# Narrowing fewer pieces of the channel weights while the first batch's attention runs alone

## The chip, the cores and the metric

One core of a Trainium2 chip runs the whole program. The metric is the device time of one execution in microseconds (us). The kernel before took 1027.16 us, the median of three runs that lay between 1025.83 and 1028.11. Its engines are TensorE (PE in the profile, with PEld for its weight loads), VectorE (DVE), ScalarE (ACT), GpSimd (POOL) and SyncE (SP), which here issues the loads and stores.

## The reference

Four batches of 576 tokens go through three layers: an attention with 8 heads of width 64 in which only scores within `tau` of the row's maximum count, a mixing layer, and a routed layer with 8 experts.

```python
scores = scale * np.matmul(q, k.transpose(0, 1, 3, 2))
thresh = np.max(scores, axis=-1, keepdims=True) - tau
scores = np.where(scores >= thresh, scores, -1000000000.0)
scores = scores - np.max(scores, axis=-1, keepdims=True)
attn = np.exp(scores)
attn = attn / (np.sum(attn, axis=-1, keepdims=True) + 1e-09)
x = np.matmul(attn, v)

h = x.transpose(0, 2, 1) @ U @ V            # mixing along the tokens
u = x + h.transpose(0, 2, 1)
x = u + np.maximum(u @ w_ch1, 0.0) @ w_ch2  # the channel layer, 512 -> 2048 -> 512
# then: each token picks an expert e, or keeps the one of the token before it
out = p[e] * (np.maximum(x @ w1[e], 0.0) @ w2[e])
```

`U`, `V`, `w_ch1` and `w_ch2` arrive as eight-byte floating-point numbers, everything else in four bytes. The change bears on `w_ch1` and `w_ch2`, which are called the channel weights here.

## The kernel before, in words

The program has stages. **Stage 0** is the attention of batch 0 by itself (`attention_alone`). **Stage 1** runs the attention of batch 1 beside the channel layer of batch 0 (`attention(1)` and `channel(0)`), stages 2 and 3 do the same for the next batches, and the routed experts come last.

In stage 0 the attention goes over 36 tiles of scores (4 pairs of heads, 9 tiles each) in a loop over `i`, from 0 to 38. For a tile, TensorE makes scores (L321, L323), VectorE finds the row maximum (L356, tile `st`), ScalarE takes the exponential (L367, tile `p`), VectorE masks (L371), TensorE transposes (L427) and ScalarE copies the result out of PSUM (L428, tile `ptt`), and TensorE multiplies with V (L446 to L450, tile `po`). The next pair of heads is loaded beside that: a load into `raw`, a cast `kh` on ScalarE (L292), a remainder `kl` (L293, on GpSimd for these pairs) and a cast `qs` (L300). Where a tile leaves TensorE idle, matmuls that compute nothing (L596, `idle`) are put in.

**Narrowing.** Matmuls need four-byte weights, so a generator `convert` turns the eight-byte numbers into four-byte ones, piece by piece. Every `next(conv)` is called a call here. A call issues the load of a new piece into `cr` (L204), casts the piece of the call before on ScalarE (L212, tile `top`) and joins the piece of two calls before on VectorE (L219, tile `w`). The join's result is stored to a buffer `wdram` in HBM (L243). There are 35 pieces: one for U, two for V, and two for each of the 16 blocks `f` of the channel weights, so that block `f` is pieces 4 + 2f and 5 + 2f. The first of the two holds the weights of the first matrix, the second those of the second. `cr` has three buffers. Casts and joins are pinned (`keep_in_program_order`): the planner can't move them on their engines. A piece that is joined has been read out of `wdram` again before it can be used: `load_w(b, f)` loads a block into `wr` (L686), splits it into a high part `w0h` or `w1h` (on ScalarE, L693, for blocks 0 and 1 of batch 0, on GpSimd, L691, for the later ones) and a low part `w0l` or `w1l` (L694, on GpSimd). `w0h` and `w0l` have two buffers.

What calls when: in stage 0 the loop over `i` keeps a `debt` that decides at which `i` a call is made. `load_w(0, f)` makes as many calls as are missing until `DONE` has reached `f`; that is the case at call 8 + 2f. In stage 1 the rest of the calls stand beside attention and channel layer in `interleave`, which lets each generator go forward by its share of the whole; the calls' share is set as if there were 30. `channel(0)` begins with `load_w(0, 0)` and `load_w(0, 1)`, computes the first layer of block 0 (`mlp_l1`, L715 to L717, tile `l`; relu L718, L719), then calls `load_w(0, 2)`, and so on. In between, after each fourth block, comes the second layer (`mlp_l2`, L730 to L732).

A planner puts the instructions of every engine in an order from the order in which they were traced and from its own estimates of what is ready when. In stage 0 GpSimd alone keeps the traced order. Loads of `wr` are often moved to well before the place where they were traced.

Of the kernel before, what the change touches and what calls it, by code (L numbers as in the profile page):

```python
# [103 lines left out]
def attention_channel_moe(ctx, tc, qk, vv, tau, umat, vrep, wch, wgl, wexp, consts, out):  # L104
# [765 lines left out]
    debt = 0  # L870
    with tc.manual_schedule(engines={mybir.EngineType.Pool}):
        for i in attention_alone(0):
            if i >= 4:
                debt += 0.2 if i > 9 else 1
                while debt > 0:
                    next(conv, None)
                    debt -= 1
# [514 lines left out]
```

## Time and profile before

| what | value |
|---|---|
| median of three runs | 1027.16 us |
| profiled execution | 1030.32 us |
| its span, first to last instruction | 1028.5 us |
| PE busy | 992.5 us (97%) |
| DVE busy | 714.4 us (69%) |
| ACT busy | 612.9 us (60%) |
| POOL busy | 156.3 us (15%) |
| TensorE's granted clock, mean | 0.996 |

The profiled execution took 1.82 us more than its span, which is the time before the first and after the last instruction. All times in rows count from the span's start. Busy time is a sum over stages that have different limits, so the shares in the table do not say which engine a stage waits for; the rows by stage do. Stage 0 ends at 109.56 us, where the first matmul of the channel layer starts, and stage 1 ends near 262 us.

### The profile page before, as it was taken

The numbers are of one execution on the slowest core, as the hardware profiler recorded it, in microseconds if no ns is written. First come the engines' busy times: TensorE is split into PE (matmuls) and PEld (weight loads), VectorE is DVE, ScalarE is ACT, GpSimd is POOL, SyncE is SP. The second block draws the span as 40 slices with busy tenths as digits, with TensorE's granted clock in tenths as the row PEclk, the third lists the DMA queues.
The fourth block names the chain that finished last, engine by engine and source line by source line (L and its number), as shares of the span: only waits on it lengthen the run. The fifth ranks groups of instructions, "written<-read, shape, count | busy, mean of one in ns | idle before, by whom it ended". The sixth has DMA issues, their size and how long they took to land.

```text
span 1028.5 us, 17792 instructions
## 1 busy us (share of the span) xinstructions
PE 992.5 (97%) x6309; PEld 831.9 (81%) x6310; DVE 714.4 (69%) x1764; ACT 612.9 (60%) x1250; POOL 156.3 (15%) x149
## 2 busy tenths in 40 slices
PE   8898999999999999999999999999999899999996
PEld 4676777778787787788889888999998798889884
DVE  7898687786777877777686655682469655566673
ACT  6888687676587776776475553432353344355562
POOL 3322345332000000000000000014400321120100
PEclk9999999999999999999999999999999999999999
DMA  7655486863332322323111011362243645565550
GB/s 229 226 157 178 155 267 222 277 213 111 121 104 95 103 86 81 114 98 99 52 58 52 33 52 39 132 234 94 82 161 144 232 147 185 173 194 197 194 184 16
DMA packets 58529, 143.72 MB, mean 140 GB/s; under 512 B 7421, under 2 KB 8573, under 8 KB 58432
## 3 DMA queue, kind: packets, MB, share of 16 engines
q1 hardware_dynamic: 55072, 132.27, 39.5%
q0 software_dynamic: 3360, 10.23, 3.0%
q8 instruction: 52, 0.85, 0.3%
q14 instruction: 45, 0.37, 0.1%
HBM read 124.65 MB, written 18.61 MB: 139 GB/s over the span
## 4 chain that ended last, share of the span: by engine, by line
PE 75%; DVE 6%; ACT 5%; DMA 4%; issue 4%; POOL 1%; SPq 0%; POOLq 0%; DVEq 0%; ACTq 0%
PE l L730 6%; PE l L732 6%; PE l L731 6%; PE l L715 6%; PE l L717 5%; PE l L716 5%; PE tp L427 4%; PE el L1211 4%; PE el L1258 3%; PE el L1257 3%; PE el L1213 3%; PE el L1256 3%; PE el L1212 3%; PE po L446 3%; PE s L321 3%
## 5 line engine op out<-in xcount | busy, mean ns | idle before, releaser
L1142 ACT ACTIVATE eh<-ew 128x512 fp32r<-128x512 f32 x160 | 94.2, 627 | 70.1 <-PE el L1258 55.5
L1143 DVE TENSOR_TENSOR el<-ew,eh 128x512 fp32r<-128x512 f32 x160 | 106.9, 692 | 40.6 <-ACT eh L1142 38.1
L371 DVE SCALAR_TENSOR_TENSOR p<-s,st,p 128x576 f32<-128x576 f32 x144 | 114.0, 815 | 19.8 <-ACT p L367 16.0
L715 PE MATMUL l<-uh,w0h 128*128 128x256 f32 (+2 forms) x352 | 126.7, 361 | 0.3 <-ACT yT L519 0.3
L367 ACT ACTIVATE p<-s,st 128x576 f32<-128x576 f32 x144 | 103.4, 738 | 32.2 <-DVE st L356 30.9
L716 PE MATMUL l<-ul,w0h 128*128 128x256 f32 (+2 forms) x352 | 122.6, 348 | 0.0
L717 PE MATMUL l<-uh,w0l 128*128 128x256 f32 (+2 forms) x352 | 122.3, 348 | 0.0
L356 DVE TENSOR_REDUCE st<-s 128x1 f32<-128x576 f32 x144 | 105.3, 751 | 16.1 <-PE s L323 15.2
L730 PE MATMUL l<-hh,w1h 128*128 128x512 f32 (+3 forms) x320 | 115.4, 361 | 0.0
L732 PE MATMUL l<-hh,w1l 128*128 128x512 f32 (+3 forms) x320 | 112.6, 352 | 0.0
L731 PE MATMUL l<-hl,w1h 128*128 128x512 f32 (+3 forms) x320 | 112.2, 351 | 0.0
L428 ACT ACTIVATE ptt<-tp 128x512 f32<-128x512 f32 (+1 forms) x192 | 88.5, 489 | 31.0 <-PE tp L427 30.6
L694 POOL TENSOR_TENSOR w1l<-wr,w1h 128x512 fp32r<-128x512 f32 x24 | 31.4, 1320 | 453.7 <-DVE rha L1000 426.2
L321 PE MATMUL s<-kh,qs 128*128 128x288 f32 x320 | 95.7, 319 | 4.6 <-DVE p L371 4.5
L427 PE MATMUL tp<-cst,p 128*128 128x128 f32 x576 | 91.7, 276 | 5.5 <-ACT ptt L428 4.2
L735 DVE TENSOR_TENSOR yT<-l,yT 128x448 f32<-128x448 f32 (+2 forms) x96 | 50.1, 522 | 58.5 <-PE l L732 57.9
L323 PE MATMUL s<-kl,qs 128*128 128x288 f32 x320 | 88.7, 296 | 0.0
L381 ACT ACTIVATE p<-p,rv 128x576 f32<-128x576 f32 x108 | 78.6, 771 | 15.9 <-DVE rv L391 15.7
L427 PEld LDWEIGHTS tp<-cst,p 128*128 128x128 f32 x576 | 68.0, 140 | 21.7 <-ACT ptt L428 10.1
L446 PE MATMUL po<-ptt,v 128*64 128x256 f32 (+1 forms) x256 | 70.2, 413 | 2.8 <-ACT ptt L435 2.0
L447 PE MATMUL po<-ptt,v 128*64 128x256 f32 (+1 forms) x256 | 70.9, 414 | 1.7 <-ACT ptt L428 1.7
L715 PEld LDWEIGHTS l<-uh,w0h 128*128 128x128 f32 x352 | 66.4, 189 | 6.7 <-DVE rsm L810 0.7
(613 smaller groups left out, 2433.5 us busy)
## 6 DMA issues: line engine op xcount, KB each, us to landing
ew<-in_wexp_dram SPq DMA_DIRECT2D x80, 512.0 KB, 4.5
wr<-wdram SPq DMA_DIRECT2D x128, 256.0 KB, 2.9
cr<-in_wch_dram SPq DMA_DIRECT2D x32, 512.0 KB, 4.8
raw<-in_qk_dram SPq DMA_DIRECT2D x30, 304.0 KB, 3.1
wdram<-w SPq DMA_DIRECT2D x32, 256.0 KB, 3.1
v<-in_vv_dram SPq DMA_DIRECT2D x16, 352.0 KB, 4.1
raw<-in_qk_dram SPq DMA_DIRECT2D x16, 320.0 KB, 3.1
raw<-in_qk_dram SPq DMA_DIRECT2D x16, 288.0 KB, 4.1
```

The source lines that it names most:

```text
L321: pe.matmul(s["t"][:, h, :288], lhsT=qs[:, qc:qc + 128], rhs=kh[:, k0:k0 + 288], start=(j == 0), stop=False)
L356: dve.tensor_reduce(out=self.st[:, 0, h:h + 1], in_=self.t[h], axis=AX.XY, op=ALU.max, negate=True)
L367: act.activation(self.halves(h), self.t[h], AF.Exp, bias=self.st[:, 0, h:h + 1])
L371: dve.scalar_tensor_tensor(out=p, in0=self.t[h], scalar=self.st[:, 1, h:h + 1], in1=p, op0=ALU.is_ge, op1=ALU.mult, accum_out=self.rvs[:, ...
L427: pe.transpose(tp[:, c - c0], src[:, c * 128:c * 128 + 128], ident)
L715: pe.matmul(pm, lhsT=w1h[:, wk], rhs=uh[k], start=(k == 0), stop=False)
L716: pe.matmul(pm, lhsT=w1h[:, wk], rhs=ul[k], start=False, stop=False)
L717: pe.matmul(pm, lhsT=w1l[:, wk], rhs=uh[k], start=False, stop=(k == 3))
L730: pe.matmul(pm, lhsT=w2h[:, wd], rhs=xh, start=(f == f0), stop=False)
L731: pe.matmul(pm, lhsT=w2h[:, wd], rhs=xl, start=False, stop=False)
L732: pe.matmul(pm, lhsT=w2l[:, wd], rhs=xh, start=False, stop=(f == f0 + 3))
L1143: dve.tensor_tensor(out=lo, in0=x, in1=hi.bitcast(F32), op=ALU.subtract)
```

## The change

The debt grows by 0.1 instead of 0.2 for each `i` above 9.

```diff
     with tc.manual_schedule(engines={mybir.EngineType.Pool}):
         for i in attention_alone(0):
             if i >= 4:
-                debt += 0.2 if i > 9 else 1
+                debt += 0.1 if i > 9 else 1
                 while debt > 0:
                     next(conv, None)
                     debt -= 1
```

Worked through, the calls of stage 0 are made before at i = 4 to 10, 15, 20, 25, 30 and 35 (12 calls), and after at i = 4 to 10, 20 and 30 (9 calls). The remaining pieces are narrowed in stage 1, by the calls in `load_w` and in `interleave`. The number of pieces and the work on each are the same.

## Rows read from the trace of the kernel before

**Rows 1.** Busy by stage: us, PE, PEld, DVE, ACT, POOL; clock, DMA, GB/s.

```profile
0.00:109.50 109.50, 94.64 (x647) 66.77 (x648) 93.82 (x229) 90.06 (x196) 32.44 (x33) 1.00 0.61 190
109.50:262.00 152.50, 146.75 (x866) 112.91 (x867) 113.30 (x238) 109.87 (x209) 59.42 (x58) 1.00 0.67 214
262.00:430.00 168.00, 167.74 (x1016) 130.37 (x1016) 128.93 (x305) 124.42 (x256) 0.00 (x0) 1.00 0.31 101
```

**Rows 2.** VectorE, joins of i = 25 and 35: start, length, instruction, [idle before].

```profile
69.74 0.68 DVE L219 SCALAR_TENSOR_TENSOR w<-cr,top 128x512 int32<-128x512 int32 x1
...
93.23 1.51 DVE L219 SCALAR_TENSOR_TENSOR w<-cr,top 128x512 int32<-128x512 int32 x1
```

**Rows 3.** ScalarE in stage 0, three casts and what follows.

```profile
47.41 0.80 ACT L212 ACTIVATE top<-cr 128x512 f16<-128x512 bf16 x1
...
70.56 0.79 ACT L212 ACTIVATE top<-cr 128x512 f16<-128x512 bf16 x1
71.21 0.67 ACT L292 ACTIVATE kh<-raw 128x576 fp32r<-128x576 f32 x1
...
76.61 0.80 ACT L300 ACTIVATE qs<-raw,t 128x608 fp32r<-128x608 f32 x1 [0.31 <-DMA raw<-in_qk_dram]
...
93.96 0.79 ACT L212 ACTIVATE top<-cr 128x512 f16<-128x512 bf16 x1
...
97.20 0.80 ACT L300 ACTIVATE qs<-raw,t 128x608 fp32r<-128x608 f32 x1 [0.35 <-DMA raw<-in_qk_dram]
```

**Rows 4.** TensorE from 47 us on.

```profile
47.43 0.43 PE L447 MATMUL po<-ptt,v 128*64 128x256 f32 x1 [1.35 <-ACT ptt L428]
...
52.10 0.71 PE L427 MATMUL tp<-cst,p 128*128 128x128 f32 x5
```

**Rows 5.** The chain of waits: start, length, what.

```profile
71.96 1.43 POOL kl L293
...
73.40 3.18 DMA raw<-in_qk_dram
...
82.52 2.47 DMA wdram<-w
...
85.00 5.79 DMA wr<-wdram
...
92.79 1.42 POOL kl L293
```

**Rows 6.** VectorE as stage 1 begins.

```profile
110.35 0.75 DVE L671 TENSOR_TENSOR ul<-yT,uh 128x256 fp32r<-128x256 f32 x2
...
113.98 1.58 DVE L219 SCALAR_TENSOR_TENSOR w<-cr,top 128x512 int32<-128x512 int32 x2
```

**Rows 7.** Transfers issued in 115:135: KB each, median us to landing.

```profile
cr<-in_wch_dram SPq DMA_DIRECT2D x5, 512.0 KB, 4.3
wdram<-w SPq DMA_DIRECT2D x5, 256.0 KB, 3.1
wr<-wdram SPq DMA_DIRECT2D x4, 256.0 KB, 3.3
```

**Rows 8.** GpSimd, the first block split in stage 1.

```profile
112.42 0.61 POOL L691 CAST w0h<-wr 128x512 fp32r<-128x512 f32 x1 [16.25 <-PE l L716]
113.11 1.30 POOL L694 TENSOR_TENSOR w0l<-wr,w0h 128x512 fp32r<-128x512 f32 x1
```

**Rows 9.** TensorE around the layer of block 2.

```profile
116.69 0.40 PE L715 MATMUL l<-uh,w0h 128*128 128x512 f32 x1
...
117.81 0.48 PE L716 MATMUL l<-ul,w0h 128*128 128x512 f32 x1
...
120.41 0.27 PE L427 MATMUL tp<-cst,p 128*128 128x128 f32 x1
...
123.43 0.70 PE L450 MATMUL po<-ptt,v 128*128 128x256 f32 x2
```

**Rows 10.** Busy time of the first 20 us of stage 1.

```profile
110.00:130.00 20.00, 19.69 (x111) 15.59 (x110) 11.62 (x25) 13.43 (x25) 9.84 (x10) 1.00 0.61 196
```

## The prediction

> **What bounds the kernel now.** I read the busy time by stage first [rows 1], because shares over the whole span mix stages with different limits. The reader is to see three things there. In stage 0 no engine is full: of 109.5 us PE is busy 94.64, DVE 93.82 and ACT 90.06, so the stage is a chain that passes from engine to engine, and an instruction taken out of one of them pays only where the chain runs through it. In stage 1 PE is busy 146.75 of 152.5 us, so 5.75 us are idle and the stage is nearly PE's own. From 262 to 430 us PE is busy 167.74 of 168.0. What stage 0 and stage 1 win or lose together therefore arrives at the end, and nothing later gives it back.
>
> Then I read VectorE and ScalarE around the removed joins and casts [rows 2, 3], TensorE beside one of them [rows 4], the chain of waits through the second half of stage 0 [rows 5], and finally what stands at the start of stage 1 [rows 6 to 10], because that is where the moved pieces arrive.
>
> **What the change removes from stage 0.** Before, calls are made at i = 15, 20, 25, 30 and 35; after, at 20 and 30. Each call holds one cast and one join, so three casts and three joins leave. By place they are those of i = 15, 25 and 35; what stands at 20 and 30 stays there, on an earlier piece. A cast holds ScalarE for 0.65 us (70.56 to 71.21), a join VectorE for 0.68 [rows 2, 3].
>
> - i = 15: the cast at 47.41 lies beside TensorE, which starts at 47.43 on a PSUM copy and then runs through to the transposes at 52.10 [rows 3, 4]. The chain is on TensorE there, so I count nothing. Its cover gone, it would be the cast's 0.65.
> - i = 25: the cast at 70.56 stands directly ahead of the cast `kh` at 71.21, and behind that come `kl` on GpSimd (71.96, 1.43 us), the load of `raw` (73.40, 3.18 us) and the cast `qs` at 76.61, before which ScalarE sat idle for 0.31 us on that load [rows 3, 5]. If the whole run moves up by 0.65, `qs` is 0.31 earlier for certain, and more if the copies ahead of it move too. I take 0.5.
> - i = 35: the cast and the join lie at 93.96 and 93.23, but `qs` at 97.20 again waited for a load, which waits for the `kl` that starts at 92.79, ahead of both [rows 3, 5]. What is late next is that load, so the gain is small; I take 0.2.
>
> Stage 0 thus gives back 0.7 us. The bounds are 0, if all of it falls into waits, and three casts of 0.65 with joins of 0.68, 0.68 and 1.51, together 4.8 us. I stay near the lower end because two of the three places have a row that shows something else ending last.
>
> The join at 93.23 took 1.51 us where the one at 69.74 took 0.68, and `kl` ran on GpSimd from 92.79 to 94.21 beside it [rows 2, 5]. The Trainium skill has a rule for this (SBUF — State Buffer, Who interferes with whom): a DVE instruction with two inputs in SBUF contends with a GpSimd instruction that reads SBUF. It speaks against the change, since GpSimd is busy 32.44 of 109.5 us in stage 0 and 9.84 of 20 us where the pieces go [rows 1, 10]. By that rule the first moved join would take 0.83 us longer when it meets GpSimd, and the sum below would be 1028.8; without it, it is 1028.0.
>
> **What it adds to stage 1.** The three casts and three joins come back in its first 20 us: 2.0 us for each engine. DVE is idle for 8.4 and ACT for 6.6 of these 20 us [rows 10], so the work itself costs nothing; PE is busy for 19.69, so what counts is whether it is kept waiting. GpSimd's splits, the stores and the loads are the same in number.
>
> The weights come later. `load_w(0, 1)` needs call 10 and finds nine, so it makes one, and that call joins piece 8, the first half of block 2. Before, call 10 stood at i = 25, near 70 us. Now it stands behind `mix(0)`, whose last remainders `ul` end on VectorE at 111.10 [rows 6]. Shifted by the 0.7 from stage 0, that is 110.4. Then come the join (0.68), the store to HBM (3.1), the load back (3.3) and the split on GpSimd (112.42 to 114.41, 1.99) [rows 7, 8]: 119.5. The layer of block 2 issued its first matmul at 116.69 and the rest from 117.81 on [rows 9]; shifted, 117.1. The weights come 2.4 us late. The store took 2.47 and a load 5.79 in the chain [rows 5], which makes it 1.7 to 4.9.
>
> What hides part of it: the transposes and the product with V that run from 120.41 to 124.13 [rows 9] could go ahead of block 2, if the planner orders them so and the copies that they read are there. Whole cover would leave 0, no cover 4.9. I take 1.5 of the 2.4: the product's own inputs are copied while the wait lasts, so not all of it can move up.
>
> Behind that the schedule meets the old one. In `interleave` the calls get one turn for each 1/30 of the stage; before, `load_w(0, 4)` finds 16 calls made, as it needs, and after it finds 15 and makes one. From block 5 on the counts are the same, so blocks 3 and 4 are the last that can be late. Their pieces are joined before the layers of blocks 1 and 2, a block or two ahead, so I count 0 for them.
>
> A pinned cast can also hold up ScalarE. The buffer of piece 11 is freed by the join of call 10, at about 111.1, and its load takes 4.3 us [rows 7], so its cast can't start before 115.4, while its place, in call 12, is close behind block 0. Behind it queue the exponentials of batch 1 and the relus, for which TensorE and VectorE wait. ScalarE's 6.6 idle us cover it; if not, it costs up to 2.
>
> **The sum.** -0.7 + 1.5 = +0.8. Against the profiled execution's own time, 1028.5 of span and 1.82 around it, that is 1030.32 + 0.8 = 1031.1; the median of the runs is 3.16 us below that execution, so the median should be 1027.16 + 0.8 = 1028.0. About 0.2% (2.05 us) is what a measurement of this kernel can tell from no change, so this is within 1025.1 to 1029.2.
>
> **Rivals.**
>
> *Stalled at the head of stage 1 (slower).* The planner leaves block 2 where it was. TensorE takes its instructions in order, so the whole lateness is idle time. For: a load took 5.79 us in the chain [rows 5], and PE has 0.31 idle us in these 20 [rows 10]. Against: in stage 1 as a whole PE has 5.75 idle us [rows 1], part of which attention work done early can fill. It decides once the weights come later than the product with V can cover. Price: 4.9 - 0.7 = +4.2, so 1031.4.
>
> *Stage 0 pays in full (faster).* If the chain is carried by ScalarE and VectorE at all three places, and block 2 is covered, the gain is up to 4.8; with half of what the bound leaves above my 0.7 it is 0.7 + 2.05 = 2.75, so 1024.4. For: at 71.21 and 97.20 ScalarE waits by only 0.31 and 0.35 for loads [rows 3], so the two paths are almost equally long, and the moved work goes to engines that have 8.4 and 6.6 us free. Against: TensorE's run from 47.43 and the load chain.
>
> *It does nothing.* `load_w` makes missing calls, and loads of `wr` are moved early anyhow; if the store and load were never waited for and the casts were hidden, the time is 1027.2.
>
> **Chances and range.** Forecast 0.42, stall 0.27, full gain in stage 0 0.24, nothing 0.07. The range takes the bounds: 1027.16 - 4.8 = 1022.4 with nothing lost in stage 1, and 1027.16 + 4.9 = 1032.1 with nothing won in stage 0; the likeliest case's own range is 1025.9 to 1029.9. Faster by over 0.2%: most of the full gain, and a little of the forecast, 0.25. Slower: most of the stall and the upper end of the forecast, 0.31. Within: 0.44.
>
> **What would show it.** The changed profile should have eight casts and seven joins before stage 1 instead of eleven and ten, counting those of U and V; the first matmul of the channel layer near 108.9 instead of 109.56; a join of a channel piece right behind the last `ul`, a load of `wr` at about 114, GpSimd's split of block 2 ending near 119.5, and a wait of TensorE's line L715 for GpSimd's `w0l`, which the profile before hardly has. The forecast is wrong if stage 0 ends more than 2 us earlier, if L715 waits more than 4 us, or if the difference arises behind block 5, where the calls are the same in number.

## The result and the profile after

The kernel after took 1035.28 us, the median of seven runs (1032.19 to 1035.59), beside 1027.16 for the kernel before in seven runs of its own (1025.25 to 1030.60). The ratio on record is 1.0067 with a 95% interval of 1.0051 to 1.0082: slower by 6.9 us, at least 5.2 and at most 8.4. It is worked out from all the runs; the two medians alone differ by 8.1 us, which lies in that interval too. The prediction had 1028.0 and a range up to 1032.1. It is wrong, and on the slow side.

The busy time by stage, of the kernel after, answers to [rows 1]; columns as there.

```profile
0.00:109.50 109.50, 93.85 (x639) 66.16 (x639) 89.78 (x223) 86.21 (x188) 30.18 (x31) 1.00 0.51 161
109.50:262.00 152.50, 142.86 (x836) 110.83 (x835) 111.02 (x235) 108.49 (x203) 63.27 (x60) 0.99 0.69 227
262.00:430.00 168.00, 167.73 (x1003) 130.09 (x1001) 128.67 (x303) 124.13 (x250) 0.00 (x0) 1.00 0.31 99
```

In the first stretch VectorE and ScalarE have some 4 us less than before, partly because the cut at 109.5 us now falls 3.7 us ahead of the stage's end. In the second stretch PE is busy 3.89 us less than before, in the same 152.5 us, of which the first 3.7 still belong to stage 0: it waits. The third stretch is full, as before, so nothing is won back there.

**The end of stage 0.** VectorE in the profile after, from 107 to 113 us (start, length, instruction, idle time before); it answers to [rows 6].

```profile
108.03 0.67 DVE L219 SCALAR_TENSOR_TENSOR w<-cr,top 128x512 int32<-128x512 int32 x1
108.62 0.75 DVE L356 TENSOR_REDUCE st<-s 128x1 f32<-128x576 f32 x1
...
109.74 0.82 DVE L371 SCALAR_TENSOR_TENSOR p<-s,st,p 128x576 f32<-128x576 f32 x1
...
110.59 0.29 DVE L505 TENSOR_TENSOR th<-rep,th 64x128 fp32r<-64x128 f32 x1
...
112.46 0.43 DVE L671 TENSOR_TENSOR ul<-yT,uh 128x256 fp32r<-128x256 f32 x1 [0.47 <-ACT uh L670]
```

The join at 108.03 is that of call 10, the call which `load_w(0, 1)` makes because the loop left one too few. The prediction had put it behind the last `ul`. The planner put it in the middle of the last mixing steps, ahead of a row maximum that the next score tile needs, and TensorE, in the same profile, waits 0.88 us for the mask that follows (before, 0.3 at the most in these steps):

```profile
110.62 0.49 PE L321 MATMUL s<-kh,qs 128*128 128x288 f32 x1 [0.88 <-DVE p L371]
...
113.22 0.63 PE L715 MATMUL l<-uh,w0h 128*128 128x512 f32 x1
113.65 0.63 PE L716 MATMUL l<-ul,w0h 128*128 128x512 f32 x1
```

Line L715 is the first matmul of the channel layer: 113.22 instead of 109.56. The same shape took 0.50 there before and 0.63 here. The windows of the kernel after give the reason: from 111 to 114 us the granted clock is 0.50, the lower of its two levels (1.2 instead of 2.4 GHz).

```profile
111.00:114.00 3.00, 3.00 (x13) 2.89 (x13) 2.35 (x7) 1.78 (x5) 0.00 (x0) 0.50 0.65 192
114.00:117.00 3.00, 3.00 (x16) 2.46 (x15) 0.15 (x2) 1.82 (x3) 0.58 (x1) 0.97 0.05 20
```

I call the time from the first `ul` of stage 0 (VectorE, L671) to the first matmul of the channel layer the tail. It is 9.55 us before (100.01 to 109.56) and 10.97 after (102.25 to 113.22).

**The first 40 us of stage 1.** VectorE's joins after, again beside [rows 6], then the issues of SyncE's queue between 125 and 135 us, then GpSimd's splits beside [rows 8].

```profile
117.86 1.70 DVE L219 SCALAR_TENSOR_TENSOR w<-cr,top 128x512 int32<-128x512 int32 x2
...
124.06 0.69 DVE L219 SCALAR_TENSOR_TENSOR w<-cr,top 128x512 int32<-128x512 int32 x1
...
125.34 0.69 DVE L219 SCALAR_TENSOR_TENSOR w<-cr,top 128x512 int32<-128x512 int32 x1 [0.59 <-ACT top L212]
...
131.65 1.29 DVE L219 SCALAR_TENSOR_TENSOR w<-cr,top 128x512 int32<-128x512 int32 x2
```

```profile
126.45 0.47 SPq L243 DMA_DIRECT2D wdram<-w  x1
...
133.25 0.99 SPq L243 DMA_DIRECT2D wdram<-w  x1
134.29 1.51 SPq L686 DMA_DIRECT2D wr<-wdram  x2
```

```profile
116.42 0.61 POOL L691 CAST w0h<-wr 128x512 fp32r<-128x512 f32 x1 [18.27 <-PE l L716]
...
139.78 0.61 POOL L691 CAST w0h<-wr 128x512 fp32r<-128x512 f32 x1 [0.16 <-DMA wr<-wdram]
140.47 1.60 POOL L694 TENSOR_TENSOR w0l<-wr,w0h 128x512 fp32r<-128x512 f32 x1
```

Block 2 is split at 116.42, and GpSimd had waited there for TensorE to free a buffer, as before: block 2 is not late. Block 3 starts some 2 us later than before (16.2 us behind block 0 instead of 14.2), and block 4 is the late one. Its first piece is the join at 125.34, its store is issued at 126.45, but its load only at 134.29, behind the store of the joins of 131.65. It is split at 139.78, and TensorE waits. All waits of TensorE from 113 to 150 us after (line, releaser, us in total, times, longest):

```profile
PE po L446 <- ACT ptt L428: 1.3, 1, 1.3
PE l L717 <- POOL w0l L694: 1.2, 2, 0.9
PE s L321 <- DVE p L371: 1.0, 1, 1.0
PE tp L427 <- ACT p L381: 0.8, 1, 0.8
PE l L715 <- POOL w0h L691: 0.3, 1, 0.3
PE tp L427 <- ACT ptt L428: 0.2, 1, 0.2
```

and the same view of the kernel before, from 109.5 to 146 us:

```profile
PE l L715 <- ACT yT L519: 0.3, 1, 0.3
PE po L447 <- ACT ptt L428: 0.3, 1, 0.3
```

That is 4.8 us against 0.6. Only 1.5 of the 4.8 name the weights. The rest names ScalarE and VectorE. Block 4 starts 27.2 us behind block 0 instead of 19.2, so TensorE has only attention work ahead of it, and that work seems to be bound by its own copies and masks. The windows of the kernel after show where PE is not full (in the same three stretches it was busy 9.69, 9.96 and 9.18 us before):

```profile
120.00:130.00 10.00, 8.67 (x51) 6.01 (x49) 6.23 (x13) 6.85 (x14) 3.38 (x4) 1.00 0.87 289
130.00:140.00 10.00, 7.64 (x46) 5.97 (x44) 7.11 (x16) 7.32 (x13) 4.00 (x5) 1.00 0.96 302
140.00:150.00 10.00, 8.79 (x44) 6.51 (x44) 7.23 (x12) 7.72 (x17) 8.11 (x7) 1.00 0.92 334
```

Transfers issued from 118 to 145 us after, beside [rows 7] (KB each, median us to landing):

```profile
cr<-in_wch_dram SPq DMA_DIRECT2D x8, 512.0 KB, 5.6
wdram<-w SPq DMA_DIRECT2D x9, 256.0 KB, 3.5
wr<-wdram SPq DMA_DIRECT2D x7, 256.0 KB, 4.6
```

That is eight loads of new pieces and nine stores. Before, the same stretch counted from the first matmul of the channel layer (114 to 141 us) had seven and seven, and the medians were 4.7 for `cr`, 2.9 for `wdram` and 3.3 for `wr`: the bunch is one or two pieces more, and each transfer takes somewhat longer.

### The profile page after: what moved, and what is told of

It is laid out like the page before. It is cut to its first block, busy times and chain, and to the rows that moved or that the text cites. A ratio compares the mean times of both kernels' runs of the same rounds, so it can differ in the third digit from the quotient of the medians.

```text
span 1032.3 us, 17792 instructions
## 1 busy us (share of the span) xinstructions
PE 993.8 (96%) x6310; PEld 832.6 (81%) x6310; DVE 712.9 (69%) x1764; ACT 613.2 (59%) x1250; POOL 158.8 (15%) x149
## 5 line engine op out<-in xcount | busy, mean ns | idle before, releaser
L715 PE MATMUL l<-uh,w0h 128*128 128x256 f32 (+2 forms) x352 | 126.8, 361 | 0.3 <-POOL w0h L691 0.3
L321 PEld LDWEIGHTS s<-kh,qs 128*128 128x128 f32 x320 | 60.6, 189 | 18.0 <-DVE p L371 8.3
L717 PEld LDWEIGHTS l<-uh,w0l 128*128 128x128 f32 x352 | 66.6, 189 | 8.0 <-POOL w0l L694 2.1
L719 DVE SCALAR_TENSOR_TENSOR hl<-l,hh 128x512 fp32r<-128x512 f32 (+2 forms) x80 | 46.3, 579 | 38.3 <-ACT hh L718 38.0
```

Of the source, the lines that this page charges most:

```text
L321: pe.matmul(s["t"][:, h, :288], lhsT=qs[:, qc:qc + 128], rhs=kh[:, k0:k0 + 288], start=(j == 0), stop=False)
L715: pe.matmul(pm, lhsT=w1h[:, wk], rhs=uh[k], start=(k == 0), stop=False)
L717: pe.matmul(pm, lhsT=w1l[:, wk], rhs=uh[k], start=False, stop=(k == 3))
```

## The experiments

Since the prediction rests on one profile, I took more of both kernels, and read every run at the same marks. A block's start is that of its first L715 matmul, counted from that of block 0; "idle" is the time between the starts of blocks 0 and 15 less what TensorE was busy in it (a window each). All in us. The ratio is the one on record, to runs of the kernel before on the same chip, with its 95% interval; it is worked out from all the runs and differs by up to 0.13% from the quotient of the medians.

| kernel | first `ul` | tail | block 1 | block 2 | block 4 | block 15 | idle | ratio |
|---|---|---|---|---|---|---|---|---|
| before (shown) | 100.01 | 9.55 | 3.2 | 7.1 | 19.2 | 145.7 | 5.7 | 1 |
| before, 2nd profile | 101.92 | 9.55 | 3.2 | 7.1 | 19.4 | 148.4 | 7.7 | |
| before, 3rd | 103.88 | 9.55 | 3.2 | 7.1 | 19.5 | 146.4 | 6.0 | |
| after (shown) | 102.25 | 10.97 | 3.6 | 7.2 | 27.2 | 149.8 | 8.8 | 1.0067 (1.0051 to 1.0082) |
| after, 2nd | 102.83 | 11.10 | 3.4 | 7.0 | 27.0 | 151.2 | 10.1 | |
| twelve, three last | 105.05 | 12.95 | 4.1 | 9.1 | 20.9 | 146.5 | 4.9 | 1.0068 (1.0035 to 1.0102) |
| nine, other places | 102.70 | 11.10 | 3.4 | 7.1 | 27.3 | 150.9 | 9.8 | 1.0074 (1.0044 to 1.0104) |
| eleven | 102.38 | 9.55 | 3.2 | 7.1 | 19.8 | 146.4 | 5.8 | 1.0028 (0.9996 to 1.0059) |
| twelve, early | 103.18 | 9.54 | 3.2 | 7.1 | 19.5 | 146.5 | 6.2 | 1.0021 (1.0005 to 1.0036) |
| fifteen | 102.88 | 10.06 | 3.1 | 8.2 | 20.0 | 145.6 | 5.6 | 1.0057 (1.0033 to 1.0081) |
| weights given | 104.50 | 12.24 | 4.1 | 7.8 | 21.2 | 146.8 | 5.8 | |
| no pieces of blocks 2, 3 | 103.79 | 9.55 | 3.2 | 7.1 | 19.5 | 144.0 | 3.9 | |
| idle matmuls in tail | 103.29 | 10.35 | 3.2 | 6.9 | 27.2 | 150.0 | 9.0 | 1.0098 (1.0071 to 1.0126) |
| one call fewer asked | 101.76 | 9.55 | 3.2 | 13.1 | 28.0 | 151.7 | 9.0 | 1.0109 (1.0089 to 1.0129) |
| other queue | 103.61 | 10.75 | 3.9 | 7.5 | 30.5 | 167.6 | 18.6 | 1.0286 (1.0270 to 1.0303) |
| not pinned | 108.08 | 10.66 | 3.1 | 8.1 | 20.8 | 148.0 | 8.1 | 1.0106 (1.0086 to 1.0126) |

### More profiles of the same kernels

The kernel before, unchanged, twice; the kernel after, once.

> The kernel before, unchanged, for a second profile. If the profile that was shown held a wait in the expert stage that other executions don't have, the second expert's layer (L1211 y1h) ends within 22 us of its start of the first (L1211 y0h 757.9) plus 35, as in the changed kernel's profile, and the span is 1024 to 1027 us; if not, it is 1028.5 again with the wait.

> The kernel before, unchanged, for a third profile: how much stage 0 up to the first ul of mix(0) differs between executions of one kernel (100.0 and 101.9 us so far), against 102.3 to 103.8 us in the kernels with other calls. Every theory: tail 9.55 us, fifth block at 19 to 20 us.

> The changed kernel, unchanged, for a second profile: first ul at 102 to 103 us if stage 0 before its tail is really longer by one or two us, 100 to 102 if that was the execution. Late weights and tail: tail near 11 us, fifth block near 27 us, both again.

The profiled executions took 1033.71, 1029.06 and 1034.13 us. Two things follow. The tail and the starts of blocks 1 to 4 repeat within 0.3 us in each kernel, so their differences are the change's. The first `ul` does not: 100.01, 101.92 and 103.88 in one and the same kernel. The gain of 0.7 that I had worked out for stage 0 is smaller than that spread, and the profile that I worked from was the earliest of three. The kernel after, with three casts and joins fewer, is at 102.25 and 102.83, no earlier than the mean of before, 101.94.

### Where the calls stand, and how many there are

Four versions of the loop, each with the calls at given places; this is twelve calls with three of them last:

```diff
-                debt += 0.1 if i > 9 else 1
...
+            for _ in range([4, 5, 6, 7, 8, 9, 10, 20, 30, 36, 37, 38].count(i)):
+                next(conv, None)
```

> Nine calls in the loop as after the change (i = 4 to 10, 20, 30), and the three missing ones at i = 36, 37 and 38, the end of the attention alone. So stage 1 begins with as many pieces asked for as before. Theory 'late weights' (blocks 3 and 4 come too late because five pieces are narrowed in a bunch at the head of stage 1): the second layer starts within 25 us of the first matmul of the channel layer (before 23.2, after 31.4), and about 4 us of the 8 come back: ratio 1.003 to 1.005. Rival 'order' (any other set of places gives another order by the planner, and the loss has nothing to do with the weights): second layer as late as after the change, ratio near 1.007 or anything else.

Blocks 2 and 4 are nearly on time and the idle time is back to 4.9, but the first `ul` is at 105.05 and the tail 12.95. The three joins (100.26, 101.66 and 104.44 on VectorE) all stand ahead of that `ul`. What stands in the tail is a cast, and it had to wait for its piece; TensorE then waited for the copy `yT` behind it:

```profile
107.42 0.78 ACT L212 ACTIVATE top<-cr 128x512 f16<-128x512 bf16 x1 [2.01 <-DMA cr<-in_wch_dram]
109.91 0.90 PE L472 MATMUL tx<-cst,yT 128*128 128x128 f32 x3 [3.03 <-ACT yT L453]
```

From 111 to 117 us the clock is at 0.50. What stage 1 wins, the end of stage 0 loses; the ratio of 1.003 to 1.005 that I expected did not come.

Nine calls, as in the kernel after, but at 15 and 20 instead of 20 and 30:

```diff
+            for _ in range([4, 5, 6, 7, 8, 9, 10, 15, 20].count(i)):
```

> Nine calls in stage 0 as after the change, but at i = 4 to 10, 15 and 20, the places of before; the calls of i = 25, 30 and 35 are gone. Late weights: stage 1 loses as after the change, second layer 30 us or more behind the first matmul; stage 0 keeps the order of before up to i = 25 and ends 0.7 to 2 us earlier than before, so ratio 1.002 to 1.005. Rival 'order': no reason for stage 1 to be slow again; ratio within 0.3% of 1.

All marks are those of the kernel after, and the earlier end of stage 0 that I expected is not there. With nine calls it does not matter where in the loop two of them stand.

Eleven calls:

```diff
+            for _ in range([4, 5, 6, 7, 8, 9, 10, 15, 20, 25, 30].count(i)):
```

> Eleven calls: only that of i = 35 is taken away. Late weights: block 3's first half is joined in stage 1 instead of at i = 35, but the bunch is three pieces, not five or six; second layer 23 to 27 us behind the first matmul, ratio 0.998 to 1.002. Rival 'order': ratio may be anything within 1%.

The tail is 9.55 again and block 4 starts at 19.8: one wait for `w0l` of 0.6 us is left. The ratio's interval touches 1.

Twelve calls, the number of the kernel before, all by i = 15:

```diff
+            for _ in range([4, 5, 6, 7, 8, 9, 10, 11, 12, 13, 14, 15].count(i)):
```

> Twelve calls as before, pinned, but all at i = 4 to 15. Theory: no call in the tail and no late block, so tail 9.55 us, fifth block at 19 to 20 us, ratio 0.997 to 1.003, whichever side of stage 0 the calls stand on. Rival 'place' (the early part of stage 0 is less able to hide calls than the middle): the first ul of mix(0) later than 105 us and ratio over 1.004.

It has the marks of the kernel before, and its time to 0.2% (1.0021, at least 1.0005). So twelve calls by i = 15 are nearly as good as twelve spread out, and nine are not. And more calls than before, fifteen:

```diff
-                debt += 0.1 if i > 9 else 1
+                debt += 0.3 if i > 9 else 1
```

> The other direction: the debt grows by 0.3, so 15 calls in stage 0 instead of 12. If the weights' lateness at the head of stage 1 is what matters and before still has some, ratio 0.997 to 1.000; if stage 0 pays for each call, 1.001 to 1.003.

Stage 1 is as before and the tail 0.5 longer, yet the timed ratio is 1.0057, above both ranges that I expected. Its profiled execution took 1031.99 us where its median is 1035.65, so the profile doesn't show what the timed runs lose. This one stays open.

### Is it the wait for the pieces?

The kernel after, with the loads of blocks 2 to 4 (batch 0) taken from an input instead of the narrowed pieces: same loads in size and number, same casts, joins and stores, nothing to wait for. The kernel thereby leaves out the channel layer's product with these weights, and other tokens go to other experts, so only stages 0 and 1 are read; the whole time (1087.34 us) says nothing here.

```diff
-            sp.dma_start(out=x, in_=wdram[f * 128:f * 128 + 128, i * 512:i * 512 + 512])
+            sp.dma_start(out=x, in_=qk[f][:, i, 0:512] if b == 0 and f in (2, 3, 4) else
+                         wdram[f * 128:f * 128 + 128, i * 512:i * 512 + 512])
```

> The calls of after (i = 4 to 10, 20, 30; all later calls too), but for batch 0 blocks 2, 3 and 4 are loaded from the attention's input instead of the narrowed weights, so their loads wait for no piece; the channel layer's values of these blocks are not the reference's. All casts, joins and stores stay. Late weights: the fifth block of the first layer (started 27.2 us behind the first matmul after, 19.2 before) starts within 20 us again, and 3 to 4 us of the 7 go: ratio 1.003 to 1.005. Rival 'bunched work' (the casts and joins at the head of stage 1 take VectorE, ScalarE and the DMA queues from the attention, whoever waits for them): stage 1 stays as long, ratio near 1.007.

Block 4 starts at 21.2, a little above the 20 that I expected, block 15 at 146.8, and the idle time is 5.8, all near the kernel before. TensorE's waits from 113 to 152 us, of this kernel, name GpSimd no more:

```profile
PE po L446 <- ACT ptt L428: 1.4, 1, 1.4
PE s L321 <- DVE p L371: 0.9, 1, 0.9
PE rep L502 <- ACT tT L498: 0.6, 1, 0.6
```

So the wait for the pieces is what stage 1 pays for, and the casts and joins by themselves cost it nothing that shows (block 15 lies at 145.7 to 148.4 in the kernel before). The tail stays long, 12.24, with the join of call 10 still in it: that part has another cause.

The other way round, eight calls and no narrowing of blocks 2 and 3 at all (their loads in every batch, and that of block 1 in batch 0, come from an input; again only stages 0 and 1 are read, and the whole time, 1080.03 us, says nothing):

```diff
+            if f in (2, 3):
+                DONE[0] = f - 1
+                continue
```

> What stage 0 would win at best: before, with the calls of i = 20, 25, 30 and 35 taken out together with four pieces (blocks 2 and 3 are not narrowed at all and are loaded from the attention's input, as is block 1 for batch 0), so that nothing is late and nothing is moved; the channel layer's values are not the reference's. If the prediction's reading of stage 0 is right, four calls are worth about 1 us: ratio 0.998 to 1.000. If stage 0 pays for each cast and join: up to 5 us, ratio 0.995. If casts and joins there are wholly hidden: 1.000.

The tail is 9.55 and block 4 at 19.5. The first `ul` is at 103.79 with four calls fewer than before: in this one profile stage 0's body is not shorter, though a gain of 1 us could hide in the spread of 3.9.

### The half clock in the tail

The kernel after with six idle matmuls at the last mixing steps, where TensorE waited:

```diff
+        if nm == "0_3_4":
+            fill(2, "x")
...
+            tc.keep_in_program_order(pe.matmul(t, lhsT=idle[:, :128], rhs=idle, start=True, stop=True))
```

> After, plus six matmuls that compute nothing, pinned into the two gaps of TensorE near 108 us (two behind the product with U of the last pair, four behind the repeat that follows). Theory 'clock': the half clock from 110.6 to 114.4 us, which both kernels with nine calls show and before doesn't, costs 1.2 us; it stays at 1.0 here and the ratio falls by 0.1% to about 1.0055. Rival: the gap comes from the join of call 10 ahead of the last masks, the clock only follows; then the clock is 1.0 but the first matmul of the channel layer still comes at 113 us and nothing is won.

Windows of this kernel; from 111 to 114 us the kernel after had 0.50:

```profile
108.00:111.00 3.00, 2.60 (x29) 1.69 (x29) 2.86 (x8) 2.38 (x7) 0.00 (x0) 1.00 0.42 152
111.00:114.00 3.00, 2.99 (x18) 2.10 (x16) 2.44 (x8) 2.70 (x6) 0.00 (x0) 1.00 0.85 192
```

The clock stays at 1.00, the tail shrinks from 11.0 to 10.35 and block 1 comes at 3.2 again. As far as these matmuls cost nothing themselves, of the tail's 1.5 us the join costs 0.8 and the half clock 0.6 to 0.7, and 0.2 to 0.4 behind it. The timed ratio is not better (1.0098): the cure buys nothing that I can measure.

### One call fewer asked at the head

The kernel after with `DONE` set one call earlier, when the second piece of a block is joined and stored, so that `load_w(0, 1)` finds its call made:

```diff
+        if c.stop == 1024:
+            DONE[0] = f
...
-            DONE[0] = f - 1
```

> After, but a block of the channel weights counts as done when its second piece is joined, one call earlier than before, so load_w(0, 1) makes no call and the tail of stage 0 holds no cast and no join. Theory 'tail' (one call in the tail costs about 1.4 us there): from the first ul of mix(0) to the first matmul of the channel layer it is 9.6 us again instead of 10.97, and the clock stays at 1.0. Stage 1 then starts with one call less, so by 'late weights' blocks 2 to 4 are at least as late as after: fifth block 27 us or more behind the first. Net ratio 1.005 to 1.009. Rival 'order': the tail stays at 11 us whether or not a call lies in it.

The tail is 9.55: no join in it. But block 2's first piece is now the one that is missing: block 2 starts at 13.1. GpSimd in this kernel:

```profile
123.72 0.61 POOL L695 CAST w0h<-wr 128x512 fp32r<-128x512 f32 x1 [26.03 <-DMA wr<-wdram]
...
138.52 0.77 POOL L695 CAST w0h<-wr 128x512 fp32r<-128x512 f32 x1 [3.93 <-DMA wr<-wdram]
```

This is what the prediction had feared for block 2 in the kernel after. There the early join at 108.03 averts it, and pays for it in the tail.

### Another queue for the loads

The kernel after with the loads of blocks 2 on (batch 0) issued by GpSimd, so that they don't stand behind stores in SyncE's queue:

```diff
+            (pool if b == 0 and f > 1 else sp).dma_start(
```

> After, but in batch 0 the loads of blocks 2 and later out of wdram are issued from GpSimd's queue instead of SyncE's, where they stood behind stores that wait for later joins (the load for block 4 was issued at 134.3 us, 7.8 us after its piece's store at 126.5). Theory 'queue' (a part of the lateness is standing in SyncE's order): fifth block within 23 us of the first instead of 27.2, ratio 1.003 to 1.005. Rival 'pieces' (the pieces themselves are joined too late, the queue only follows the planner): fifth block at 26 to 28 us, ratio near 1.007 or worse, since GpSimd now spends time on issuing.

Far worse: block 15 at 167.6. In this kernel GpSimd itself now waits for stores before it can issue, and its splits stand behind that, in order:

```profile
123.29 0.58 POOL L686 DMA_DIRECT2D wr<-wdram  x1 [3.41 <-DMA wdram<-w]
126.65 0.54 POOL L686 DMA_DIRECT2D wr<-wdram  x1 [2.78 <-DMA wdram<-w]
```

So it doesn't tell how much of block 4's lateness is the place in SyncE's queue and how much the late joins. The kernel with eleven calls tells more, since its block 4 is on time. These are the join, the store, the load and the split of the same piece there:

```profile
122.44 0.69 DVE L219 SCALAR_TENSOR_TENSOR w<-cr,top 128x512 int32<-128x512 int32 x1
...
123.64 0.38 SPq L243 DMA_DIRECT2D wdram<-w  x1
...
127.59 0.32 SPq L686 DMA_DIRECT2D wr<-wdram  x1
...
131.03 0.61 POOL L691 CAST w0h<-wr 128x512 fp32r<-128x512 f32 x1 [1.97 <-DMA wr<-wdram]
```

In the kernel after the join comes 12.1 us behind the first matmul of the channel layer instead of 10.5, the load is issued 7.8 us behind its store instead of 4.0, and from there to the split it takes 5.5 us instead of 3.4. Of the 7.5 us by which block 4 is later there, about 1.6 are thus the join itself, 3.9 the place in SyncE's order, behind the stores of the joins of 131.65, and 2.1 the slower load. The second profile of the kernel after has nearly the same steps (12.2, 7.1 and 5.8). This is read from traces whose order differs in other places too; no run changed the place in the queue alone.

### Casts and joins not pinned

The kernel after without `keep_in_program_order` on cast and join:

```diff
-                tc.keep_in_program_order(dve.scalar_tensor_tensor(
+                (lambda _: None)(dve.scalar_tensor_tensor(
```

> After with the pins on the casts and joins of the narrowing taken away, so the planner may move them. In its order about sixteen joins of the channel weights stand ahead of the first ul of mix(0), and four more between there and the layer of block 0. Theory 'pin': blocks 3 and 4 are no longer late (fifth block within 21 us of the first, 27 after); the tail, with four joins in it, is longer than 11 us, and stage 0 before it longer by what nine more calls cost (0 if its body hides them, up to 12 us if not). Ratio 1.000 to 1.010. Rival 'number': blocks as late as after, since the calls are the same.

Block 4 is at 20.8: free to move, the planner takes the joins forward. It takes too many; fifteen stand ahead of the first `ul`, which comes at 108.08, and two more in the tail. Slower by 1.06%.

No version that I ran beats the kernel before.

## Why the prediction was wrong

**The step that failed** is "Their pieces are joined before the layers of blocks 1 and 2, a block or two ahead, so I count 0 for them", said of blocks 3 and 4. The pieces were joined behind the start of those layers. The first piece of block 3 is the second of the two joins of 117.86, and block 1 had started at 116.78. That of block 4 is the join at 125.34, and block 2 had started at 120.43; before, the same piece is the second join of 113.98, ahead of block 2 at 116.69. Stage 1 from block 0 to block 15 takes 150.5 us after (two profiles) against 146.8 before (three): 3.7 us more, and with the weights given it is 146.8. Other kernels bear it out: 150.9 and 150.0 in the two others with nine calls and the same block 4, 146.4 and 146.5 with eleven calls and with twelve early ones. For block 2 I had summed the times of a join, a store and a load, and nothing for their place in a queue; for block 4 I had not even that. The load of block 4 was issued 7.8 us behind its own store, after the stores of two later pieces. Join to split took 14.4 us for block 4 (125.34 to 139.78), where the sum of a join, a store and a load from [rows 7] is 7.1. Crowded transfers alone are not it: with eleven calls the stretch from 118 to 145 us has eight loads and seven stores too, at 5.7 and 3.6 us, and block 4 is on time. The extremes of the profiles (149.8 less 148.4, 151.2 less 145.7) leave 1.4 to 5.5 for it.

**Block 2, +1.5**: it is not late at all, 7.2 after against 7.1. The mechanism was right, as the run with one call fewer shows (13.1), but it needs call 10's join where I put it, behind the last `ul`. The planner put it at 108.03, ahead of the last two `ul` (112.46 and 113.66).

**Stage 0, -0.7**: with the tail, the sign was wrong. Ahead of the tail no run shows a gain, neither with three calls fewer nor with four, but the spread of 100.01 to 103.88 would hide one of 0.7. That the waits for `raw` [rows 3] take what the casts gave is likely, but argued; no run tells it apart. I had the 0 as a bound, and took 0.5 for the cast at i = 25. On top, the join of the forced call adds 1.4 to 1.5 us to the tail, a term that my sum didn't have. The kernels with no join in it have 9.54 or 9.55, but for two: the one with fifteen calls (10.06; its last join at 99.22 stands 3.7 us ahead of the tail) and the one with three calls last (12.95; the waiting cast). The counts show the same: ahead of stage 1 there are nine casts and eight joins, not the eight and seven that I named, because call 10's stand there too.

**The pinned cast, up to 2**: it is there. At 124.54 a cast on ScalarE had waited 1.66 us for its load of `cr`, the copy `ptt` stood behind it, and TensorE waited 1.33 for that (the first line of its waits). With the weights given the same wait is there with 1.4, and the stage is still not longer, so it seems to be covered by idle time that otherwise stands elsewhere. In the tail it is not covered: with three calls last the cast at 107.42 waited 2.01 us, and TensorE 3.03 behind it.

**The join beside GpSimd**: the rule of the Trainium skill that I weighed (SBUF — State Buffer, Who interferes with whom) agrees: the two joins at 117.86, beside the split at 117.11 to 118.41, took 1.70 us together, while 0.67 is one alone at 108.03. That is 0.4 more, half of the 0.83 that I gave it, and on an engine with time to spare; before, the two joins at 113.98 took 1.58 [rows 6], so most of it was there already.

**The sum by what was measured**: 1.5 for the tail and 3.7 for stage 1 make 5.2 of the 6.9, the lower end of the interval. By the marks behind it, the first expert's first matmul is at 765.7 and 767.8 after and 757.9, 762.9 and 762.5 before: 5.7 later in the mean, of which 0.6 stands in the body of stage 0, where one kernel varies by 3.9. The 1.2 that are left lie inside the interval, and I can't place them. The shown pair of profiles would have misled here too: their spans differ by 3.8 us, since the shown execution of before took 270.6 us from that matmul to its end, where its other two took 269.0 and 264.8.

Of the rivals, *stalled at the head of stage 1* came nearest: weights late by way of a join, a store and a load. Its place (block 2) was off. Its price, 4.9 at most, covers the 3.7 that stage 1 lost, but by luck, since it was worked out for block 2; and it had no cost in stage 0.

## What to carry to other kernels

Work taken out of a stage in which no engine is full need not make it shorter; here no gain showed. The same work, made just in time by its consumer, can land in a worse place: here in the tail of the stage, where a join cost 1.4 to 1.5 us. When producers are pushed towards their consumers, cost the whole round trip (join, store, queue, load, split) as a burst for every consumer of the next tens of us, not only for the first. Before a gain below 1 us is argued from a stage's profile, take the same kernel's profile two or three times and look which marks repeat.

## What the runs showed of the hardware that was not expected

- The granted clock fell to 0.50 behind a stretch in which TensorE was only partly busy. In the kernel with three calls last PE was busy 1.09 of the 3 us from 108 to 111, and the clock was at 0.78 there and 0.50 from 111 to 117; in the kernel after it was busy 1.48 of the same 3 us, ahead of its 0.50, and its longest single wait there was 0.88 us. In the tail before, PE was busy 1.95 us in the emptiest stretch of 3 us (105 to 108), and the clock stayed at 1.00. The kernel with three calls last, then before:

```profile
108.00:111.00 3.00, 1.09 (x5) 1.01 (x6) 1.74 (x5) 2.46 (x6) 0.00 (x0) 0.78 0.86 252
111.00:114.00 3.00, 2.90 (x26) 2.46 (x25) 1.91 (x6) 1.42 (x4) 0.00 (x0) 0.50 0.79 245
...
105.00:108.00 3.00, 1.95 (x26) 1.36 (x25) 2.83 (x9) 2.66 (x7) 0.00 (x0) 1.00 0.26 100
```

- Moving loads of 256 KB to GpSimd's queue took the ratio from 1.0067 to 1.0286, some 2.2% more, although GpSimd was busy less than half of stage 1 before [rows 1]: what it waits for before an issue, its other work waits for too.
- One kernel's stage 0 differed by 3.9 us from one execution to the next (100.01 to 103.88 at the first `ul`), while the 9.55 us behind it repeated to 0.01.
